# Projections by halves of TensorE's columns, steps ordered by use of the array, and turns split around the next scores

## The chip, the cores and the metric

The kernel runs on one core of one Trainium2 chip. The metric is the device time of one execution in microseconds (us); the time given for a kernel is the median of several executions. The profile is one execution recorded by the hardware profiler. A core has five engines that work at the same time and wait for each other through semaphores: PE (TensorE, matrix products; PEld is its loading of weights, that is of the operand that stands still), DVE (VectorE), ACT (ScalarE), POOL (GpSimd) and SP (which issues transfers here).

## The reference

Two blocks follow each other. The first is a linear attention with polynomial features, on 4 batches of 4 heads, 1088 tokens and 32 columns a head:

```python
def phi(x):
    a = np.einsum('rd,bhsd->bhsr', S1, x)
    b = np.einsum('rd,bhsd->bhsr', S2, x)
    return np.einsum('bhsi,bhsj->bhsij', a, b).reshape(*x.shape[:-1], r * r)
q_p, k_p = (phi(q), phi(k))
kv = np.einsum('bhsf,bhsd->bhfd', k_p, v)
z = np.sum(k_p, axis=2)
num = np.einsum('bhsf,bhfd->bhsd', q_p, kv)
den = np.einsum('bhsf,bhf->bhs', q_p, z)[..., None] + 1e-06
x = num / den
```

Its result, with the heads side by side, is the input `x` (4, 1088, 128) of the second block: four experts, each a causal softmax attention with 64 columns, of which a gate picks two for each token.

```python
logits = x @ w_gate
topk = np.argpartition(-logits, K, axis=-1)[..., :K]      # K = 2
w = softmax of the two picked logits
for e in range(E):                                        # E = 4
    q = x @ wq[e]; k = x @ wk[e]; v = x @ wv[e]
    scores = scale * (q @ k.transpose(0, 2, 1))           # causal mask, then softmax
    a = softmax(scores)
    ye = a @ v @ wo[e]
    out += ye * (w where e was picked, else 0)
```

All of it is computed in 32-bit floats.

## The kernel before

**The work of a batch.** The first block of a batch ("preparing" it) takes these steps, each a small function inside `prepare`: `begin` (DVE turns the loaded k and q), `sketch` (products with S1 and S2, then the features), `kvs` (features of k times v), `turn_features` (features of q turned on TensorE), `numer` (numerator and denominator, then the division on DVE into `xs`) and `turn_x` (that result turned into `xT`). From `xT` come the projections: `project` makes q or k of two experts for 512 tokens (tile `qk`), `project_tails` the same for the last 64 tokens (`qkt`), `project_v` the values and gate logits of 128 tokens (`vg`), and `gate` the weights of the experts.

**The units.** The second block of a batch is cut into eight units by `units`: a pair of blocks of 128 query tokens times a pair of experts. The first pair of blocks is one unit of kind Q; the second gives two units of kind P; the third and fourth give four of kind G; the last 64 tokens are one unit of kind L. The last batch takes them in another order, with Q at the end. A unit has up to two halves, x = 0 and x = 1, one for each block of queries. It goes through these stages:

- scores (`make(x)`, tiles `sc`): TensorE multiplies q and k; then DVE adds the mask and takes the maximum (`take`), and ACT takes exp and the sum (`soften`), which leaves the softmax in a tile `a`
- turns (`turns_of`, tiles `tp`): TensorE turns `a` in blocks of 128x128, two halves of rows at a time, and `evacuate` copies the result to `aT`
- values (`values`, tiles `av`): TensorE multiplies `aT` and the values
- output (`output`, tiles `po` and `acc`): the product with `wo`, and the weighting with the gate.

`evacuate` gives one copy of three to DVE and two to ACT. All results of TensorE go to one pool of eight PSUM banks.

**The order on TensorE is written out by hand.** The other engines are ordered by a planner; TensorE executes exactly in the order in which the loop at the end calls these functions. In each step of that loop, n counts the units of a batch, and the next batch is prepared in between: `ahead[n]` holds what is done for the next batch in this step, `own[n]` what is left of this batch's projections. Before the change a step is:

1. scores of both halves of the unit
2. output of the unit before the last
3. values of an earlier unit
4. `tiled`: steps of the preparation that stand on their own
5. the turns, with other steps (`own` and `between`) spread among them by `weave`, which uses a guessed time for each (the number that `piece` takes). For kinds G and L the turns of the unit itself are all done in the step; for Q and P they are done in the next step, and their values one step later still.

**How the array is used.** TensorE's array has 128 rows and 128 columns. Four uses occur here, and a profile shows them before the shape of the result: `128*128` (the whole array: `qk`, `qkt`, `vg`), `64*128` (two halves of the rows, which work on two products side by side: `sc`, `tp`, `tq`, `tx`, `po`), `128*64` (two halves of the columns: `av`, `kv`) and `64*64` (quarters: `kps`, `qps`, `num`, and the scores of kind L). Where two products go to two halves, their instructions stand one after the other and run at the same time.

Of the kernel before, what the change touches and what calls it, by code (L numbers as in the profile page):

```python
# [19 lines left out]
def kernel(  # L20
# [20 lines left out]
    nc = tc.nc  # L41
    B, H, S, D = q.shape
    R = S1.shape[0]
    DM, E = w_gate.shape
    HD = wq.shape[2]
    assert (H, D, R, E, HD, S) == (4, 32, 8, 4, 64, 1088) and H * D == DM == 128
    C = S // 32
    NJ = (S + 127) // 128
    SP = 128 * NJ
    NG = E // 2  # L50
# [36 lines left out]
    kT = const("kT", [128, SP])  # L87
    qT = const("qT", [128, SP])
# [127 lines left out]
    def prepare(b):  # L216
        first = b == 0
# [137 lines left out]
            for _ in range(n):  # L355
                nc.tensor.matmul(t, idle, idle[:, None, :].to_broadcast([128, 4, 128]), start=True, stop=True)

        def wt(a):
            return wqk[:, a // NG, 2 * (a % NG) : 2 * (a % NG) + 2, :].rearrange("p e d -> p (e d)")

        def project(a, c):
            t = bank(f"qk{b}_{a}_{c}")
            nc.tensor.matmul(t, wt(a), xT[:, 512 * c : 512 * c + 512], start=True, stop=True)  # L363
            evacuate(qk[:, a, 512 * c : 512 * c + 512], t)

        def project_tails():
            t = bank(f"qkt{b}")
            for a in range(2 * NG):
                nc.tensor.matmul(t[:, 64 * a : 64 * a + 64], wt(a), xT[:, 1024:S], start=True, stop=True)
            evacuate(qk[:, :, 1024:], t[:, 0 : 64 * 2 * NG].rearrange("p (a s) -> p a s", a=2 * NG))  # L370

        def project_v(j):
            m = size(j)
            t = bank(f"vg{b}_{j}")
            nc.tensor.matmul(t[0:m, 0 : E * HD + E], xT[:, 128 * j : 128 * j + m], wvg, start=True, stop=True)  # L375
            evacuate(vt[0:m, j], t[0:m, 0 : E * HD + E])

        def gate(j0, j1):
# [21 lines left out]
            nc.vector.tensor_tensor(out=w, in0=w, in1=tops, op=ALU.mult)  # L400


        def piece(us, f, *args):
            return us, lambda: f(*args)

        halves = ((0, 4), (4, NJ))
        sk, sq = ([piece(0.13 * (j1 - j0), sketch, nm, t, j0, j1) for j0, j1 in halves] for nm, t in (("k", kT), ("q", qT)))
        kv = [piece(2.2, lambda: (kvs(0), kvs(1)))]
        tq = [piece(0.06 * n, turn_features, y, min(y + n, 2 * NJ)) for n in ((4 if first else 8),) for y in range(0, 2 * NJ, n)]
        nu = [piece(0.25 * (x1 - x0), numer, x0, x1) for x0, x1 in (((0, 4), (4, NJ)) if first else ((0, 5), (5, NJ)))]  # L410
        cuts = ((0, 2), (2, 4), (4, 7), (7, NJ)) if first else ((0, 5), (5, NJ))
        tx = [piece(0.06 * (x1 - x0), turn_x, x0, x1) for x0, x1 in cuts]
        vg = [piece(0.43, project_v, j) for j in range(NJ)] + [piece(0.0, gate, 0, NJ)]
        pr = [[piece(0.86, project, a, c) for a in (0, 2, 1, 3)] for c in range(2)]
        pr[1].append(piece(0.8, project_tails))
        turn_in = [piece(0.0, begin), piece(0.0, begin_rest)]


        if first:

            ahead = turn_in + sk + [piece(0.0, busy, 1)] + sq[0:1] + kv + tq[0:2] + nu[0:1]
            ahead += [piece(0.0, load_next, 0)] + sq[1:] + [piece(0.0, load_next, 1)] + tx[0:2]
            ahead += pr[0][0:3] + tq[2:5] + pr[0][3:4]
            own = [nu[1:] + vg[0:4] + tx[2:] + [piece(0.0, load_next, 2)], vg[4:] + pr[1][0:1], pr[1][1:4], pr[1][4:]]
        else:
            tiled = [turn_in + sk + sq, [], kv, [], [], nu, [], []]
            if b == 1:
                tiled[0:4] = [[], [], turn_in + sk, sq + kv]
            between = [[], [], [], [], tq, [], tx + vg[0:6], vg[6:] + pr[0]]
            ahead = list(zip(tiled, between))  # L430
            own = [pr[1][0:2], pr[1][2:3], pr[1][3:4], pr[1][4:]] if b < B - 1 else [pr[1][0:2], pr[1][2:]]
        return (qk, vt, gw), ahead, own


# [97 lines left out]
        return r  # L532


    def weave(jobs, fillers):

        n, spent, total = max(len(jobs), 2), 0.0, sum(us for us, _ in fillers)
        fillers = collections.deque(fillers)
        for s in range(n):
            if s < len(jobs):  # L540
                jobs[s]()
            while fillers and (s == n - 1 or spent + fillers[0][0] / 2 <= total * (s + 1) / n):
                us, f = fillers.popleft()
                spent += us
                f()

    def units(b, qk, vt, gw):

        for p in range((NJ - 1) // 2) if b < B - 1 else (1, 3, 2, 0):
            yT = p2.tile([128, NG, 256], F32, tag="yT", name=f"yT{b}_{p}")
            z = p4.tile([128, 2, E], F32, tag="z", name=f"z{b}_{p}")
            nk = 2 * (2 * p + 2)
            four = []
            for g in range(NG):
                if p or not g:
                    aT_all = p2.tile([128, 16 * 256], F32, tag="aT", name=f"aT{b}_{p}_{g}")
                aT = aT_all[:, 0 if p else g * nk * 256 :][:, 0 : nk * 256].rearrange("p (e j s) -> p e j s", e=2, s=256)  # L560
                name = f"{b}_{p}_{g}"

                def values(p=p, g=g, aT=aT, yT=yT, z=z, name=name):
                    av = bank(f"av{name}")
                    for j in range(2 * p + 2):
                        lo = 128 * max(0, j - 2 * p)
                        for e in range(2):
                            c = HD * (2 * g + e)
                            nc.tensor.matmul(av[HD * e : HD * e + HD, lo:256], vt[:, j, c : c + HD],  # L569
                                             aT[:, e, j, lo:256], start=(j == 0), stop=(j == 2 * p + 1))  # L570

                    evacuate(yT[:, g], av[:, 0:256])
                    if g < NG - 1:
                        return []
                    share = shares(f"{b}_{p}", z, gw[:, 2 * p : 2 * p + 2])
                    return [lambda: output(b, p, yT, share)]

                def make(x, p=p, g=g, z=z):
                    return scores(b, 2 * p + x, g, qk, z[:, x, 2 * g : 2 * g + 2])

                def turns(made, x, p=p, aT=aT, name=name):
                    return turns_of(f"{name}_{x}", 2 * p + x, made[x], aT, 128 * x)

                if p == 0:
                    four.append((turns, values))
                else:
                    yield "P" if p == 1 else "G", make, turns, [values]
            if four:
                yield ("Q", lambda x, z=z: scores_first(b, qk, [z[:, :, 2 * g : 2 * g + 2] for g in range(NG)]),
                       lambda made, x: [f for g in range(NG) for i in range(2) for f in four[g][0](made[0][g], i)],  # L590
                       [values for _, values in four])
            if p == NJ // 2 - 1:
                yield last_unit(b, qk, vt, gw)
# [50 lines left out]
    with tc.manual_schedule(engines={mybir.EngineType.PE}):  # L644
# [2 lines left out]
        for _ in range(4):  # L647
            nc.tensor.matmul(warm, idle, idle[:, None, :].to_broadcast([128, 4, 128]), start=True, stop=True)
        now, ahead, own = prepare(0)
        for _, f in ahead:  # L650
            f()

        turns, turning, groups, done = [], [], [], []

        def do_values():
            nonlocal groups
            made = [f for values in groups for f in values()]
            groups = []
            return made

        for b in range(B):
            coming, ahead, later = prepare(b + 1) if b + 1 < B else (None, [], [])
            for n, (kind, make, turned, close) in enumerate(units(b, *now)):
                tiled, between = ahead[n] if n < len(ahead) else ([], [])
                made = {x: make(x) for x in ((0, 1) if kind in "PG" else (0,))}

                for f in done:
                    f()
                done = do_values()
                for _, f in tiled:  # L670
                    f()
                jobs = turns
                turns = [f for x in made for f in turned(made, x)]
                if kind in "GL":
                    jobs += turns[: len(turns) // 2]
                weave(jobs, (own[n] if n < len(own) else []) + between)
                groups += turning
                turning = []
                if kind in "GL":
                    for f in turns[len(turns) // 2 :]:  # L680
                        f()
                    turns = []
                (groups if kind in "GL" else turning).extend(close)
            now, own = coming, later
        for f in done + turns:
            f()
        groups += turning
        for f in do_values():
            f()


# [28 lines left out]
```

## Time and profile before

| what | value |
|---|---|
| time, median of 3 | 352.77 us (352.61 to 353.52) |
| span of the profiled execution | 348.0 us |
| PE busy | 324.6 us (93%), 4970 matmul instructions |
| DVE busy | 245.4 us (71%) |
| ACT busy | 236.7 us (68%) |
| POOL busy | 45.7 us (13%) |
| mean granted TensorE clock | 0.991 |

In the profile a group of instructions is named by its line, engine and operation, and by its tiles as output<-inputs. The product of two 32-bit operands is recorded as two matmul instructions, so `x8` of `qk` are four projections. The ends of matmuls are modelled and the next one begins before the end that is shown; what a matmul takes of TensorE's time is read from the distance of starts, or from the chain of waits, where a piece runs from the start of its first instruction to the start of what follows.

### The profile page before, as it was taken

The numbers are of one execution on the slowest core, as the hardware profiler recorded it, in microseconds if no ns is written. First come the engines' busy times: TensorE is split into PE (matmuls) and PEld (weight loads), VectorE is DVE, ScalarE is ACT, GpSimd is POOL, SyncE is SP. The second block draws the span as 40 slices with busy tenths as digits, with TensorE's granted clock in tenths as the row PEclk, the third lists the DMA queues.
The fourth block names the chain that finished last, engine by engine and source line by source line (L and its number), as shares of the span: only waits on it lengthen the run. The fifth ranks groups of instructions, "written<-read, shape, count | busy, mean of one in ns | idle before, by whom it ended". The sixth has DMA issues, their size and how long they took to land.

```text
span 348.0 us, 11952 instructions
## 1 busy us (share of the span) xinstructions
PE 324.6 (93%) x4970; PEld 227.0 (65%) x4970; DVE 245.4 (71%) x856; ACT 236.7 (68%) x637; POOL 45.7 (13%) x60
## 2 busy tenths in 40 slices
PE   7998999999899899999999999999989998999973
PEld 4755558777667567677665847777765655667663
DVE  6568988779457965877766756677946766767763
ACT  2447767875767576877756875986576776857782
POOL 4001047000000821000000280000000010000000
PEclk9999999999999989999999999999999999999998
DMA  7361522200000000000000000000000000000001
GB/s 206 51 179 35 180 64 83 67 4 17 16 2 3 17 6 2 18 3 18 2 17 2 11 9 6 17 2 2 18 18 3 2 15 6 3 2 17 18 7 30
DMA packets 11383, 10.22 MB, mean 29 GB/s; under 512 B 3648, under 2 KB 10304, under 8 KB 11328
## 3 DMA queue, kind: packets, MB, share of 16 engines
q1 hardware_dynamic: 11312, 9.45, 10.0%
q8 instruction: 39, 0.64, 0.8%
q14 instruction: 16, 0.13, 0.1%
q10 hardware_dynamic: 16, 0.00, 0.0%
HBM read 7.22 MB, written 2.23 MB: 27 GB/s over the span
## 4 chain that ended last, share of the span: by engine, by line
PE 54%; DVE 21%; ACT 15%; issue 9%; DMA 0%; DVEq 0%; ACTq 0%
ACT a L442 11%; PE tp L80 10%; PE sc L455 10%; PE av L569 9%; PE qk L363 8%; DVE a L437 7%; PE vg L375 4%; DVE acc L634 3%; PE po L629 2%; PE sc L496 2%; ACT acc L633 2%; PE kv L304 2%; DVE xs L338 2%; DVE aT L69 2%; PE av L609 2%
## 5 line engine op out<-in xcount | busy, mean ns | idle before, releaser
L442 ACT ACTIVATE a<-a,mx 128x256 f32<-128x256 f32 (+8 forms) x136 | 107.5, 791 | 57.5 <-DVE mx L437 57.4
L437 DVE CUSTOM_DVE_ANT_0 a<-sc,mask 128x512 f32<-128x512 f32 (+3 forms) x136 | 74.4, 592 | 13.5 <-PE sc L455 10.9
L71 ACT COPY aT<-tp 128x512 f32<-128x512 f32 (+5 forms) x146 | 61.7, 501 | 10.8 <-PE tp L80 10.1
L569 PE MATMUL av<-aT,vt 128*64 128x256 f32 (+1 forms) x640 | 67.5, 362 | 0.4 <-DVE aT L69 0.4
L80 PE MATMUL tp<-ident,a 64*128 64x64 f32 x1296 | 59.6, 229 | 8.6 <-ACT acc L633 2.6
L80 PEld LDWEIGHTS tp<-ident,a 64*128 64x128 f32 x1296 | 49.0, 138 | 26.8 <-issue 4.8
L455 PE MATMUL sc<-qkT 64*128 64x512 f32 (+3 forms) x320 | 65.3, 534 | 0.3 <-DVE acc L634 0.3
L569 PEld LDWEIGHTS av<-aT,vt 128*64 128x64 f32 x640 | 43.4, 137 | 25.9 <-DVE mx L437 3.4
L455 PEld LDWEIGHTS sc<-qkT 64*128 64x128 f32 x320 | 33.8, 191 | 20.0 <-issue 10.3
L640 POOL TENSOR_TENSOR ob<-acc 128x256 f32<-128x256 f32 (+1 forms) x19 | 12.7, 669 | 249.2 <-DVE acc L634 69.9
L69 DVE COPY aT<-tp 128x512 f32<-128x512 f32 (+6 forms) x70 | 36.4, 547 | 11.8 <-PE tp L80 11.3
L437 DVE CUSTOM_DVE_ANT_0 a<-sc,mask,mx 128x512 f32<-128x512 f32 (+3 forms) x72 | 38.2, 568 | 0.0
L634 DVE SCALAR_TENSOR_TENSOR acc<-po,r,acc 128x128 f32<-128x128 f32 (+1 forms) x72 | 20.4, 339 | 19.6 <-ACT acc L633 18.7
L363 PE MATMUL qk<-xT,wqk 128*128 128x512 f32 x64 | 32.0, 620 | 0.7 <-ACT xT L71 0.5
L442 ACT ACTIVATION_READ_ACCUMULATOR a<-a,mx 128x1 f32 x136 | 25.4, 186 | 0.0
L629 PEld LDWEIGHTS po<-wo,yT 64*128 64x128 f32 (+1 forms) x288 | 20.2, 181 | 6.1 <-issue 2.4
L375 PE MATMUL vg<-wvg,xT 128*128 128x260 f32 (+1 forms) x72 | 19.8, 403 | 2.8 <-DVE xT L69 1.8
L633 ACT ACTIVATE acc<-po,r 128x128 f32<-128x128 f32 (+1 forms) x72 | 20.6, 356 | 2.4 <-PE po L629 2.4
L629 PE MATMUL po<-wo,yT 64*128 64x128 f32 (+1 forms) x288 | 21.6, 278 | 0.4 <-ACT yT L71 0.4
L71 ACT COPY qkT<-qk 128x512 f32<-128x512 f32 x19 | 11.1, 586 | 12.9 <-PE qk L363 12.7
L529 DVE TENSOR_SCALAR r<-z 128x8 f32<-128x8 f32 x16 | 2.7, 171 | 22.0 <-ACT a L442 22.0
L437 DVE DVE_READ_ACCUMULATOR2_ANT mx<- 128x1 f32 x216 | 17.8, 83 | 0.0
(119 smaller groups left out, 329.3 us busy)
## 6 DMA issues: line engine op xcount, KB each, us to landing
kin<-in_k_dram SPq DMA_DIRECT2D x4, 544.0 KB, 3.7
qin<-in_q_dram SPq DMA_DIRECT2D x4, 544.0 KB, 4.7
vin<-in_v_dram SPq DMA_DIRECT2D x16, 128.0 KB, 4.5
out_dram<-ob SPq DMA_DIRECT2D x15, 128.0 KB, 1.8
vtl<-in_v_dram SPq DMA_DIRECT2D x8, 16.0 KB, 2.3
wqk<-in_moe_wq_dram SPq DMA_DIRECT2D x1, 128.0 KB, 4.8
wqk<-in_moe_wk_dram SPq DMA_DIRECT2D x1, 128.0 KB, 3.5
wvg<-in_moe_wv_dram SPq DMA_DIRECT2D x1, 128.0 KB, 3.4
```

Source lines behind the costliest of these rows:

```text
L69: nc.vector.tensor_copy(out_, in_)
L71: nc.scalar.copy(out_, in_)
L80: nc.tensor.transpose(ts[half][0 : in_.shape[1], 64 * x : 64 * x + 64], in_[rows], ident[rows, rows])
L363: nc.tensor.matmul(t, wt(a), xT[:, 512 * c : 512 * c + 512], start=True, stop=True)
L375: nc.tensor.matmul(t[0:m, 0 : E * HD + E], xT[:, 128 * j : 128 * j + m], wvg, start=True, stop=True)
L437: nc.vector.tensor_tensor_reduce(out=dst, in0=src, in1=msk, scale=-1.0, scalar=most, op0=ALU.add, op1=ALU.min, accum_out=mx)
L442: nc.scalar.activation(out=a, in_=a, func=ACTF.Exp, bias=mx, scale=-1.0, accum_out=z)
L455: nc.tensor.matmul(sc[e], qk[rows, g, 128 * i : 128 * i + 128], qk[rows, NG + g, keys], start=True, stop=True)
L569: nc.tensor.matmul(av[HD * e : HD * e + HD, lo:256], vt[:, j, c : c + HD], aT[:, e, j, lo:256], start=(j == 0), stop=(j == 2 * p + 1))
L629: nc.tensor.matmul(pos[e][:, x, g], yT[rows, g, 128 * x : 128 * x + nq], wo_sb[rows, g], start=True, stop=True)
L633: nc.scalar.activation(out=acc[:, x, g], in_=pos[0][:, x, g], func=ACTF.Copy, scale=s0)
L634: nc.vector.scalar_tensor_tensor(out=acc[:, x, g], in0=pos[1][:, x, g], scalar=s1, in1=acc[:, x, g], op0=ALU.mult, op1=ALU.add)
```

## The change

It has three parts.

- **Projections by halves of the columns.** `project`, `project_tails` and `project_v` made one product that used the whole array. Each is now two products that use one half of the columns each: for `qk` and `qkt` one per expert (64 columns of weights), for `vg` one per 64 tokens. They use the array as the values (`av`) do.
- **Steps ordered by use of TensorE.** The guessed times and `weave` are gone. Each step of the loop now has four lists: `tiled` (steps that use quarters), `cols` (steps that use halves of the columns; they stand just ahead of the values), `rows` (steps that use halves of the rows; ahead of the second scores) and `rows_last` (the same, after the first turns). Thus steps of one use stand together. Several steps move for this: for later batches `numer` goes from after the values to before them; `turn_x` goes ahead of the second scores, and `project_v` after them; `kvs` moves to `cols`.
- **A unit's turns split around the next scores.** The first half of a unit's turns is done at the end of its own step, the second half in the next step, between that unit's scores of x = 0 and of x = 1. This holds for all kinds of unit, and values always follow one step after the scores.

```diff
         def project(a, c):
             t = bank(f"qk{b}_{a}_{c}")
-            nc.tensor.matmul(t, wt(a), xT[:, 512 * c : 512 * c + 512], start=True, stop=True)
+            for e in range(2):
+                nc.tensor.matmul(t[64 * e : 64 * e + 64], wqk[:, a // NG, 2 * (a % NG) + e],
+                                 xT[:, 512 * c : 512 * c + 512], start=True, stop=True)
             evacuate(qk[:, a, 512 * c : 512 * c + 512], t)
...
             for a in range(2 * NG):
-                nc.tensor.matmul(t[:, 64 * a : 64 * a + 64], wt(a), xT[:, 1024:S], start=True, stop=True)
+                for e in range(2):
+                    nc.tensor.matmul(t[64 * e : 64 * e + 64, 64 * a : 64 * a + 64], wqk[:, a // NG, 2 * (a % NG) + e],
+                                     xT[:, 1024:S], start=True, stop=True)
...
             t = bank(f"vg{b}_{j}")
-            nc.tensor.matmul(t[0:m, 0 : E * HD + E], xT[:, 128 * j : 128 * j + m], wvg, start=True, stop=True)
+            for x in range(0, m, 64):
+                nc.tensor.matmul(t[x : x + 64, 0 : E * HD + E], xT[:, 128 * j + x : 128 * j + x + 64], wvg,
+                                 start=True, stop=True)
...
-            tiled = [turn_in + sk + sq, [], kv, [], [], nu, [], []]
+            ahead = {4: ([], [], [], tq), 5: (nu, [], [], []), 6: ([], vg[0:6], tx, []), 7: ([], vg[6:] + pr[0], [], [])}
             if b == 1:
-                tiled[0:4] = [[], [], turn_in + sk, sq + kv]
-            between = [[], [], [], [], tq, [], tx + vg[0:6], vg[6:] + pr[0]]
-            ahead = list(zip(tiled, between))
-            own = [pr[1][0:2], pr[1][2:3], pr[1][3:4], pr[1][4:]] if b < B - 1 else [pr[1][0:2], pr[1][2:]]
+                ahead.update({2: (turn_in + sk, [], [], []), 3: (sq, kv, [], [])})
+            else:
+                ahead.update({0: (turn_in + sk + sq, [], [], []), 2: ([], kv, [], [])})
+            own = {0: pr[1][0:2], 1: pr[1][2:3], 2: pr[1][3:4], 3: pr[1][4:]} if b < B - 1 else {0: pr[1][0:2], 1: pr[1][2:]}
+            own = {n: ([], f, [], []) for n, f in own.items()}
...
-                made = {x: make(x) for x in ((0, 1) if kind in "PG" else (0,))}
-
+                tiled, cols, rows, rows_last = (x + y for x, y in zip(own.get(n, none), ahead.get(n, none)))
+
+                made = {0: make(0)}
+                for f in turns + rows:
+                    f()
+                if kind in "PG":
+                    made[1] = make(1)
                 for f in done:
                     f()
-                done = do_values()
-                for _, f in tiled:
+
+                for f in tiled + cols:
                     f()
-                jobs = turns
+                done = [f for values in group for f in values()]
+                group = values
                 turns = [f for x in made for f in turned(made, x)]
-                if kind in "GL":
-                    jobs += turns[: len(turns) // 2]
-                weave(jobs, (own[n] if n < len(own) else []) + between)
-                groups += turning
-                turning = []
-                if kind in "GL":
-                    for f in turns[len(turns) // 2 :]:
-                        f()
-                    turns = []
-                (groups if kind in "GL" else turning).extend(close)
+                n = (len(turns) + 1) // 2
+                for f in turns[0:n] + rows_last:
+                    f()
+                turns = turns[n:]
```

More of the change, by code (lines that the diff above doesn't have):

```diff
@@ L356, in busy @@
                 nc.tensor.matmul(t, idle, idle[:, None, :].to_broadcast([128, 4, 128]), start=True, stop=True)
-        def wt(a):
-            return wqk[:, a // NG, 2 * (a % NG) : 2 * (a % NG) + 2, :].rearrange("p e d -> p (e d)")
         def project(a, c):
             t = bank(f"qk{b}_{a}_{c}")
-            nc.tensor.matmul(t, wt(a), xT[:, 512 * c : 512 * c + 512], start=True, stop=True)
+            for e in range(2):
+                nc.tensor.matmul(t[64 * e : 64 * e + 64], wqk[:, a // NG, 2 * (a % NG) + e],
+                                 xT[:, 512 * c : 512 * c + 512], start=True, stop=True)
             evacuate(qk[:, a, 512 * c : 512 * c + 512], t)
@@ L400, in gate, with piece @@
             nc.vector.tensor_tensor(out=w, in0=w, in1=tops, op=ALU.mult)
-        def piece(us, f, *args):
-            return us, lambda: f(*args)
+        def piece(f, *args):
+            return lambda: f(*args)
         halves = ((0, 4), (4, NJ))
-        sk, sq = ([piece(0.13 * (j1 - j0), sketch, nm, t, j0, j1) for j0, j1 in halves] for nm, t in (("k", kT), ("q", qT)))
-        kv = [piece(2.2, lambda: (kvs(0), kvs(1)))]
-        tq = [piece(0.06 * n, turn_features, y, min(y + n, 2 * NJ)) for n in ((4 if first else 8),) for y in range(0, 2 * NJ, n)]
@@ L410, in prepare @@
-        nu = [piece(0.25 * (x1 - x0), numer, x0, x1) for x0, x1 in (((0, 4), (4, NJ)) if first else ((0, 5), (5, NJ)))]
-        cuts = ((0, 2), (2, 4), (4, 7), (7, NJ)) if first else ((0, 5), (5, NJ))
[L412 to L415, printed above, removed]
@@ L416, in prepare @@
-        turn_in = [piece(0.0, begin), piece(0.0, begin_rest)]
+        sk, sq = ([piece(sketch, nm, t, j0, j1) for j0, j1 in halves] for nm, t in (("k", kT), ("q", qT)))
+        kv = [piece(kvs, 0), piece(kvs, 1)]
+        many = 4 if first else 8
+        tq = [piece(turn_features, y, min(y + many, 2 * NJ)) for y in range(0, 2 * NJ, many)]
+        nu = [piece(numer, x0, x1) for x0, x1 in (((0, 4), (4, NJ)) if first else ((0, 5), (5, NJ)))]
+        cuts = ((0, 2), (2, 4), (4, 7), (7, NJ)) if first else ((0, 5), (5, NJ))
@@ L419, in prepare @@
+        tx = [piece(turn_x, x0, x1) for x0, x1 in cuts]
+        vg = [piece(project_v, j) for j in range(NJ)] + [piece(gate, 0, NJ)]
+        pr = [[piece(project, a, c) for a in (0, 2, 1, 3)] for c in range(2)]
+        pr[1].append(project_tails)
+        turn_in = [begin, begin_rest]
         if first:
-            ahead = turn_in + sk + [piece(0.0, busy, 1)] + sq[0:1] + kv + tq[0:2] + nu[0:1]
-            ahead += [piece(0.0, load_next, 0)] + sq[1:] + [piece(0.0, load_next, 1)] + tx[0:2]
+            ahead = turn_in + sk + [piece(busy, 1)] + sq[0:1] + kv + tq[0:2] + nu[0:1]
+            ahead += [piece(load_next, 0)] + sq[1:] + [piece(load_next, 1)] + tx[0:2]
@@ L423, in prepare @@
             ahead += pr[0][0:3] + tq[2:5] + pr[0][3:4]
-            own = [nu[1:] + vg[0:4] + tx[2:] + [piece(0.0, load_next, 2)], vg[4:] + pr[1][0:1], pr[1][1:4], pr[1][4:]]
+            own = {0: (nu[1:], vg[0:4], [], tx[2:] + [piece(load_next, 2)]), 1: ([], vg[4:] + pr[1][0:1], [], []),
+                   2: ([], pr[1][1:4], [], []), 3: ([], pr[1][4:], [], [])}
         else:
-            tiled = [turn_in + sk + sq, [], kv, [], [], nu, [], []]
+            ahead = {4: ([], [], [], tq), 5: (nu, [], [], []), 6: ([], vg[0:6], tx, []), 7: ([], vg[6:] + pr[0], [], [])}
@@ L532, in shares @@
         return r
[L535 to L544, printed above, removed]
-                f()
     def units(b, qk, vt, gw):
@@ L649 @@
         now, ahead, own = prepare(0)
-        for _, f in ahead:
+        for f in ahead:
             f()
[L653 to L659, printed above, removed]
-        for b in range(B):
-            coming, ahead, later = prepare(b + 1) if b + 1 < B else (None, [], [])
-            for n, (kind, make, turned, close) in enumerate(units(b, *now)):
-                tiled, between = ahead[n] if n < len(ahead) else ([], [])
-                made = {x: make(x) for x in ((0, 1) if kind in "PG" else (0,))}
+        turns, group, done = [], [], []
+        none = ([], [], [], [])
+        for b in range(B):
+            coming, ahead, later = prepare(b + 1) if b + 1 < B else (None, {}, {})
+            for n, (kind, make, turned, values) in enumerate(units(b, *now)):
+                tiled, cols, rows, rows_last = (x + y for x, y in zip(own.get(n, none), ahead.get(n, none)))
[4 more added lines that the diff above has]
+                    made[1] = make(1)
                 for f in done:
                     f()
-                done = do_values()
-                for _, f in tiled:
-                    f()
-                jobs = turns
+                for f in tiled + cols:
+                    f()
+                done = [f for values in group for f in values()]
+                group = values
                 turns = [f for x in made for f in turned(made, x)]
-                if kind in "GL":
-                    jobs += turns[: len(turns) // 2]
-                weave(jobs, (own[n] if n < len(own) else []) + between)
-                groups += turning
-                turning = []
-                if kind in "GL":
-                    for f in turns[len(turns) // 2 :]:
-                        f()
-                    turns = []
-                (groups if kind in "GL" else turning).extend(close)
+                n = (len(turns) + 1) // 2
+                for f in turns[0:n] + rows_last:
+                    f()
+                turns = turns[n:]
             now, own = coming, later
@@ L686 @@
             f()
-        groups += turning
-        for f in do_values():
+        for f in [f for values in group for f in values()]:
             f()
```

## The prediction
> **What bounds the kernel now.** I read the busy shares first, then the busy times by stretch, then the chain of waits in order of time, the groups of instructions, and last what TensorE itself waited for.
>
> ```profile
> PE 324.6 (93%) x4970; PEld 227.0 (65%) x4970; DVE 245.4 (71%) x856; ACT 236.7 (68%) x637; POOL 45.7 (13%) x60
> ...
> PE 54%; DVE 21%; ACT 15%; issue 9%; DMA 0%; DVEq 0%; ACTq 0%
> ```
>
> The chain goes through PE for 54% of the span. DVE and ACT have 30% of slack each. That alone doesn't say that PE is the bound everywhere, so here are stretches of about one batch (columns: the stretch, its length, busy us of each engine with the count of instructions, the granted clock, the share of DMA, GB/s):
>
> ```profile
> 0.00:20.00 20.00, 16.38 (x460) 11.68 (x461) 13.13 (x39) 6.54 (x20) 3.63 (x23) 1.00 0.50 117
> 20.00:113.00 93.00, 89.65 (x1344) 62.11 (x1342) 70.30 (x249) 65.11 (x182) 13.31 (x11) 1.00 0.21 60
> 113.00:197.00 84.00, 80.02 (x1240) 55.66 (x1238) 60.09 (x210) 58.63 (x161) 13.15 (x11) 0.98 0.03 9
> 197.00:278.00 81.00, 78.13 (x1170) 56.00 (x1161) 55.85 (x196) 58.02 (x149) 11.83 (x9) 1.00 0.03 9
> 278.00:348.00 70.00, 60.44 (x786) 41.56 (x782) 46.02 (x166) 48.40 (x129) 3.80 (x6) 0.98 0.04 12
> ```
>
> PE lacks 3.4, 4.0 and 2.9 us in the three middle stretches, but 9.6 us in the last one, where no batch is left to be prepared and nothing fills the waits for a softmax. In all it lacks 23.4 us. So a saving on PE in the first three batches should nearly all reach the end; in the last one less. The chain of waits shows what a visit to one kind of product costs (start, length, what):
>
> ```profile
> 91.57 1.10 PE vg L375 x4
> 93.25 1.95 PE vg L375 x8
> 127.57 1.45 PE av L569 x16
> 131.61 1.05 PE qk L363 x2
> 187.52 3.63 PE qk L363 x8
> 199.98 1.91 PE qk L363 x4
> ```
>
> For `qk` the lengths 1.05, 1.91 and 3.63 us for 2, 4 and 8 instructions lie on a line: 0.43 us each and 0.19 us for the visit. For `vg`: 0.213 each and 0.25 a visit. The 0.2 us is paid whenever the use of the array changes. I also took distances of starts from the instructions in order of time: a `qk` starts 429 ns after the one before it, but the first `tp` after the last `qk` starts 523 ns after it, which is 94 ns more; the second `qk` of a visit starts 534 ns after the first, 105 ns more. The same 94 to 98 ns stand at nearly every change of use; the second extra is 104 ns for `qk`, `vg`, `sc` and `po`, about 52 ns for `tp`, `av` and `qps`, and 25 ns for `num` and `kv`. So a change costs 200, about 150 or about 120 ns by what comes first after it.
>
> ```profile
> L569 PE MATMUL av<-aT,vt 128*64 128x256 f32 x512 | 61.9, 384 | 0.4 <-DVE aT L69 0.4
> L369 PE MATMUL qkt<-xT,wqk 128*128 128x64 f32 x32 | 4.3, 278 | 0.0
> ```
>
> One `av` instruction lasts 384 ns as recorded, yet sixteen pass in 1.45 us: two halves of the columns run side by side (by the 429 ns for 512 columns, a pair over 256 takes 213 ns and one over 128 takes 107; six such pairs and two make 1.5 us). The last view is what PE waited for:
>
> ```profile
> PE tp L80 <- ACT acc L633: 2.6, 5, 0.8
> PE vg L375 <- DVE xT L69: 1.8, 2, 0.9
> PE tp L80 <- ACT yT L71: 1.6, 1, 1.6
> PE tp L80 <- DVE xs L338: 1.3, 5, 0.4
> ...
> PE vg L375 <- ACT xT L71: 1.1, 1, 1.1
> PE tp L80 <- DVE mx L437: 1.1, 2, 0.8
> ...
> PE tp L80 <- DVE den L335: 0.5, 3, 0.2
> PE tx L80 <- ACT acc L633: 0.4, 2, 0.2
> ```
>
> [...]
>
> **Part 1 and 2: halves of the columns, and fewer changes of use.** I wrote out the order of products of both kernels and counted changes among the four uses. Before: 134. Into the whole array 31 (x 200 ns = 6.2 us), into halves of the columns 30 (28 `av` x 147, 2 `kv` x 123 = 4.4), into halves of the rows 58 (48 turns x 150, 10 `sc`/`po` x 200 = 9.2), into quarters 15 (x 120 to 147 = 2.0). Sum 21.7 us. After: 93. Whole array 1 (the idle product of the start, 0.2), columns 36 (5.3), rows 41 (39 turns, 2 others: 6.3), quarters 15 (2.0). Sum 13.7 us. Saved: 8.0 us of PE time.
>
> The products themselves cost the same: two `qk` halves over 512 columns side by side take the 429 ns of one whole (taken from `av`, where a pair over 256 columns takes 213 ns). The exception is `qkt`: its 64 columns need 53 ns but follow each other by 112 ns, as each needs a load of 128 columns of weights. With 64 columns the pair can follow by 58 ns, as the `av` of the L unit do: 32 x 54 ns = 1.7 us saved. [...] I take 1.7. The number of evacuations doesn't change. Sum of PE work saved: 9.7 us.
>
> What of it reaches the end: the three middle stretches have 3 to 4 us of waits in over 80, so nearly all there; the last (70 us) and the start (20 us) have waits that swallow most. By share that is about three quarters: 7.3 us.
>
> **Part 3 and the moved steps: waits.**
> - `vg` waits for `xT`, three times, 2.9 us in all. After, the second scores (four products, 1.7 us) and often an output (1.0 us) stand between `turn_x` and `project_v`, and a copy takes 0.5 us. Gone: 2.9 us. The wait of `tx` for a bank (0.4 us) goes too.
> - `tp` behind `numer`'s DVE work (`xs`, `den`, 1.8 us): after, an `av` of 1.3 to 2.6 us stands between. I take half: 0.9 us.
> - `tp` waiting for a softmax or for banks held by outputs (`acc`, `yT`, `mx`, 5.3 us): mostly last batch, where one wait that ends at 295.3 us is 1.6 us, and others around the last Q unit are 0.8 and 0.4 us. There the turns of a half now come after the other half's scores, an output or values, so the softmax has 3 to 5 us rather than 1 to 3. Half: 2.7 us.
> - Around 116 to 127 us DVE is the bound (9.05 us busy of 11; it turns the next batch's inputs while maxima are due), PE starves and its clock falls to a mean of 0.85 there, a loss of 1.6 us. The order of DVE's work hardly changes there; I count half of the clock loss as given back, 0.8 us.
> - New waits: at a Q step `sketch` now comes ahead of the L unit's values, not after them. Its banks need ACT, which then does eight exps and four `acc` (109.5 to 114.1 us, without a gap). Up to 1 us in each of two batches, of which the values, now later, give part back. Also the copies of a second half of turns queue on DVE behind four maxima (4 x 0.6 = 2.4 us); who waits for them is the values, and the second scores and output (1.7 + 1.0 us) lie between, except in the last batch after L. I charge 1.5 us in all.
>
> Waits net: 2.9 + 0.4 + 0.9 + 2.7 + 0.8 - 1.5 = 6.2 us. Total 7.3 + 6.2 = 13.5 us, and 352.8 - 13.5 = 339.3 us.
>
> **Rivals.**
> - *Only the changes of use pay (22%).* Waits move rather than go: DVE and ACT have as much to do, in a shorter time. For it: DVE and ACT are at 70% and would rise to 73%. Against: the `xT` wait is one of order alone. Time 352.8 - 7.3 = 345.5 us.
> - *More comes back (8%).* The even spread of maxima and exps takes most of PE's 23.4 us of lack away, except for the 6 us of start: waits give 11 us, and all of the 9.7 arrives, 332 us.
> - *Slower (8%).* [...] copies of the turns behind four maxima hold banks, and the second scores wait for a bank. With 0.5 us in each of the 32 unit steps that is 16 us against 7.3 us: 361 us. Against: eight banks are four for scores and four for turns, and the scores' banks are free once the maxima are done.
> - *Halves of the columns don't overlap (2%).* 32 `qk` x 2 x 429 ns and 32 `vg` x 2 x 219 ns more, 41 us: 387 us with the savings. The `av` rows speak against it.
>
> **How the numbers follow.** The forecast has 60%, the others 22, 8, 8 and 2. The low end takes in most of the "more" case (333), the high end the first rival with a term of new waits of 3.5 us (349). Slower by over 0.3%: the last two less what ends near no change, 8%. Within 0.3%: 3%, a part of the first rival with more new waits. Faster: 89%.
>
> **What would show it.** The distance of starts of `qk` pairs should stay at 429 ns, and of `vg` pairs at 219 ns; changes of use should still cost 94 ns each; `qkt` should fall from 112 to about 58 ns a step. The waits of `vg` for `xT` should be gone, and PE should lack some 16 us rather than 23. The middle stretches should be about 3 us shorter each for work and 1 us for waits. It is wrong if PE's lack grows, with `sc` or `tp` released by DVE's copies of `aT`, or with `qps` or `qk` waiting in the Q steps.

## The result and the profile after

The changed kernel takes 370.82 us (median of 4, 366.55 to 371.35) against 352.69 us before: a ratio of 1.0508, with a 95% interval of 1.0401 to 1.0614. It is 5% slower. The prediction was 339.3 us, with a range of 333 to 349. Some executions of a kernel ran at a lower granted clock and took over 1.5% longer than its fastest (two of five of e4_explate, the profiled one among them, and two of four of e6_warm); the ratios leave these out.

The page of the changed kernel, busy times and shares of the chain by engine:

```profile
PE 333.4 (90%) x5130; PEld 231.5 (63%) x5130; DVE 247.3 (67%) x856; ACT 233.0 (63%) x637; POOL 45.8 (12%) x60
...
PE 62%; ACT 13%; DVE 12%; issue 12%; DMA 0%; POOLq 0%; DVEq 0%; ACTq 0%
```

DVE and ACT have the same work as before within 4 us. PE is busy for 8.8 us longer although its products should be cheaper, and it lacks 35.2 us of the span (368.6 less 333.4), where it lacked 23.4 before and the prediction expected 16. Busy time by stretch shows where. The stretches run from one L unit's first scores to the next, so that both kernels are cut at the same work (columns as in the prediction). First the kernel before:

```profile
0.00:96.30 96.30, 89.33 (x1600) 62.91 (x1600) 72.32 (x237) 60.49 (x170) 16.95 (x34) 1.00 0.31 81
96.30:179.70 83.40, 79.42 (x1206) 55.14 (x1204) 59.16 (x208) 58.43 (x158) 13.15 (x11) 0.98 0.03 9
179.70:261.50 81.80, 78.93 (x1212) 57.35 (x1208) 56.27 (x204) 58.64 (x157) 11.83 (x9) 1.00 0.03 9
261.50:307.30 45.80, 44.24 (x508) 27.75 (x506) 31.96 (x105) 32.21 (x75) 1.17 (x2) 1.00 0.02 5
307.30:348.00 40.70, 32.70 (x464) 23.86 (x460) 25.68 (x105) 26.95 (x81) 2.63 (x4) 0.97 0.06 16
```

Then the changed kernel:

```profile
0.00:98.80 98.80, 90.62 (x1620) 61.42 (x1620) 72.09 (x235) 58.19 (x167) 16.95 (x34) 0.98 0.30 79
98.80:185.50 86.70, 80.03 (x1250) 56.09 (x1248) 59.65 (x208) 57.61 (x158) 13.10 (x11) 0.98 0.03 9
185.50:269.40 83.90, 79.93 (x1250) 56.17 (x1248) 57.08 (x204) 56.88 (x158) 11.89 (x9) 0.98 0.03 9
269.40:316.50 47.10, 44.34 (x552) 29.35 (x550) 32.78 (x110) 32.96 (x79) 1.74 (x3) 1.00 0.02 5
316.50:368.60 52.10, 38.47 (x480) 28.52 (x476) 25.66 (x102) 27.33 (x79) 2.07 (x4) 0.89 0.04 12
```

Every stretch is longer, by 2.5, 3.3, 2.1, 1.3 and 11.4 us, which is the whole 20.6 us between the two profiled executions. More than half is in the last stretch, from the last L unit to the end, where PE is idle for 13.6 us rather than 8.0 and its clock is granted at 0.89 rather than 0.97. What PE waited for in the changed kernel (us in total, times, longest):

```profile
PE av L563 <- ACT aT L71: 11.8, 5, 3.9
PE po L623 <- ACT aT L71: 3.4, 4, 1.1
PE sc L462 <- ACT aT L71: 2.6, 3, 1.7
PE qps L272 <- ACT aT L71: 2.0, 2, 1.0
PE num L330 <- ACT aT L71: 1.4, 2, 0.7
```

All of these end with a copy of turns (`aT`) on ACT. In the same view of the kernel before, such a copy ends one wait of 0.2 us. The waits of `vg` for `xT` are gone as forecast, and so are those of `tp` for a softmax or a bank, of which half was forecast; this took their place.

The longest of these waits, instructions in order of time (start, length, engine, line, and in brackets the idle time before and what ended it):

```profile
316.53 2.06 PE L503 MATMUL sc<-qkT 64*64 64x512 f32 x24
...
317.66 0.69 DVE L444 CUSTOM_DVE_ANT_0 a<-sc,mask 128x512 f32<-128x512 f32 x1 [0.80 <-PE sc L503]
...
318.53 1.21 PE L80 MATMUL tp<-ident,a 64*128 64x64 f32 x32
...
320.45 0.28 DVE L444 CUSTOM_DVE_ANT_0 a<-sc,mask_last,mx 128x64 f32<-128x64 f32 x1
320.61 1.20 ACT L449 ACTIVATE a<-a,mx 128x1088 f32<-128x1088 f32 x1 [3.01 <-DVE mx L444]
...
320.66 1.28 DVE L69 COPY aT<-tp 128x512 f32<-128x512 f32 x2
...
321.81 1.19 ACT L449 ACTIVATE a<-a,mx 128x1088 f32<-128x1088 f32 x1
...
322.99 1.05 ACT L71 COPY aT<-tp 128x512 f32<-128x512 f32 x2
...
323.61 2.02 PE L563 MATMUL av<-aT,vt 128*64 128x256 f32 x7 [3.87 <-ACT aT L71]
```

Read it from the end. `av` waits 3.87 us for the first of two copies on ACT. The turns that they copy were done by 319.7 us. But ACT's order has the two exps of the L unit first. These need the maxima, which DVE makes from six pieces until 320.7 us. So ACT stands idle for 3.01 us with an exp at its head that cannot start, then does both exps, and only then, from 322.99 us on, the copies. The first copy starts 4.46 us after the turns do; in e4_explate below it starts 0.78 us after them. Of these 3.7 us, 1.3 go to the wait for the maxima and 2.4 to the two exps.

Just before this wait ends the granted clock falls to 0.50. Busy time and clock (the last number but two) around it, and two visits of `av` in the chain of waits, the one before the wait and the one after it:

```profile
319.00:330.00 11.00, 7.13 (x55) 4.86 (x52) 3.76 (x15) 3.43 (x6) 0.00 (x0) 0.69 0.00 0
323.00:329.00 6.00, 5.39 (x25) 3.63 (x27) 0.81 (x5) 1.04 (x3) 0.00 (x0) 0.50 0.00 0
```

```profile
312.20 3.39 PE av L563 x32
323.61 6.67 PE av L563 x31
```

A mean of 0.69 over 11 us is 6.8 us at half speed (in the trace from 322.84 to 329.66 us), and the `av` that waited takes 6.67 us where the one before it takes 3.39.

### The profile page after: what moved, and what is told of

It reads as the page before. It is cut to its first block, busy times and chain, and to the rows that moved or that the text cites. A ratio compares the mean times of both kernels' runs of the same rounds, so it can differ in the third digit from the quotient of the medians.

```text
span 368.6 us, 12267 instructions
## 1 busy us (share of the span) xinstructions
PE 333.4 (90%) x5130; PEld 231.5 (63%) x5130; DVE 247.3 (67%) x856; ACT 233.0 (63%) x637; POOL 45.8 (12%) x60
## 4 chain that ended last, share of the span: by engine, by line
PE 62%; ACT 13%; DVE 12%; issue 12%; DMA 0%; POOLq 0%; DVEq 0%; ACTq 0%
PE av L563 17%; ACT a L449 9%; PE sc L462 9%; PE qk L361 8%; PE tp L80 8%; DVE a L444 4%; PE po L623 4%; PE vg L377 3%; ACT aT L71 3%; PE num L330 2%; PE av L603 2%; PE sc L503 2%; PE kv L304 2%; PE tq L80 1%; PE kps L272 1%
## 5 line engine op out<-in xcount | busy, mean ns | idle before, releaser
L563 PE MATMUL av<-aT,vt 128*64 128x256 f32 (+1 forms) x640 | 74.5, 377 | 14.2 <-ACT aT L71 11.8
L462 PE MATMUL sc<-qkT 64*128 64x512 f32 (+3 forms) x320 | 80.3, 558 | 3.2 <-ACT aT L71 2.6
L563 PEld LDWEIGHTS av<-aT,vt 128*64 128x64 f32 x640 | 51.8, 143 | 38.0 <-ACT aT L71 15.1
L71 ACT COPY aT<-tp 128x512 f32<-128x512 f32 (+6 forms) x143 | 60.4, 478 | 16.2 <-PE tp L80 15.5
L69 DVE COPY aT<-tp 128x512 f32<-128x512 f32 (+6 forms) x73 | 39.1, 552 | 34.1 <-PE tp L80 33.9
L80 PE MATMUL tp<-ident,a 64*128 64x64 f32 x1296 | 53.9, 225 | 0.4 <-DVE aT L69 0.2
L462 PEld LDWEIGHTS sc<-qkT 64*128 64x128 f32 x320 | 35.3, 192 | 21.9 <-issue 6.9
L361 PE MATMUL qk<-xT,wqk 128*64 128x512 f32 x128 | 33.4, 623 | 0.5 <-ACT xT L71 0.5
L71 ACT COPY yT<-av 128x256 f32<-128x256 f32 (+1 forms) x25 | 9.0, 361 | 32.0 <-PE av L563 27.0
L623 PE MATMUL po<-wo,yT 64*128 64x128 f32 (+1 forms) x288 | 25.6, 284 | 3.4 <-ACT aT L71 3.4
L377 PE MATMUL vg<-wvg,xT 128*64 128x260 f32 x136 | 18.2, 391 | 0.0
```

The costliest lines, as they stand in the source:

```text
L69: nc.vector.tensor_copy(out_, in_)
L71: nc.scalar.copy(out_, in_)
L80: nc.tensor.transpose(ts[half][0 : in_.shape[1], 64 * x : 64 * x + 64], in_[rows], ident[rows, rows])
L361: nc.tensor.matmul(t[64 * e : 64 * e + 64], wqk[:, a // NG, 2 * (a % NG) + e], xT[:, 512 * c : 512 * c + 512], start=True, stop=True)
L377: nc.tensor.matmul(t[x : x + 64, 0 : E * HD + E], xT[:, 128 * j + x : 128 * j + x + 64], wvg, start=True, stop=True)
L462: nc.tensor.matmul(sc[e], qk[rows, g, 128 * i : 128 * i + 128], qk[rows, NG + g, keys], start=True, stop=True)
```

## The experiments

Each ratio is against the kernel before on the same chip.

**Halves of the columns alone (e1_halves).** The three functions of the first hunks of the diff, in the kernel before; nothing else.

> The kernel before with the projections by halves of the columns alone; order, weave and turns as before. If the halves cost what I worked out (no more time for the products, less at each change of use, qkt without its wait for weights): changes of use fall from 22.9 to 20.0 us by count, qkt gives 1.7 us, so about 348 to 350 us against 352.7. If the halves themselves are what costs time (the rival: they do not overlap fully, or twice the instructions hold PE up): above 355 us.

Measured: 345.26 us, ratio 0.9895 (0.9843 to 0.9947). The kernel before took 349.28 us on that chip, so the gain is about 3.7 us, against 4.6 us by count (22.9 - 20.0 + 1.7; the prediction had 21.7 us for the kernel before, the count made for this run 22.9). The halves are a gain, of about the size worked out; the rival, that the halves themselves cost time, does not hold.

**The whole array again, in the changed kernel (e2_whole).** The same three functions put back, in the changed kernel.

> The changed kernel with the projections put back to the whole array; order and split as changed. Theory 'split': the exps of the next unit stand ahead of the copies of the second half of turns on ACT, and values wait; the time stays with the changed kernel, plus about 5 us for the changes of use that come back (13.7 to 19.0 us by count) and 1.7 us for qkt, so 372 to 378 us. Rival 'halves': well below the changed kernel, 360 us or less.

Measured: 373.55 us, ratio 1.0666 (1.0618 to 1.0714). This is slower than the changed kernel, by about 5.5 us if both ratios are taken at 350 us, where 7 were expected. So the loss is not in the halves. The five waits of `av` for `aT` on ACT are there as well, 11.0 us in all.

**No split (e3_nosplit).** All turns of a unit in its own step; the order by use stays.

```diff
-                n = (len(turns) + 1) // 2
+                n = len(turns)
```

> The changed kernel with all turns of a unit done in its own step: no turns between the scores, everything else as changed. Theory 'split': the waits of av for ACT's aT copies (11.8 us) fall to 2 us or less, the clock stays at full speed in most places, and the time falls below that of the kernel before, to 338 to 347 us. Rival 'moved steps' (the order by use, with values, sketch and numer in new places, is what costs): it stays above 360 us.

Measured: 340.92 us, ratio 0.9759 (0.9723 to 0.9796). One line turns 5.1% slower into 2.4% faster. In its waits of PE no copy `aT` on ACT is left:

```profile
PE qps L272 <- ACT acc L627: 3.7, 2, 1.8
PE tp L80 <- ACT acc L627: 3.0, 5, 0.7
PE tp L80 <- ACT a L449: 2.3, 6, 0.6
```

The split costs 7.5% of the time before, some 26 us; the rest of the change is worth 2.4%, of which the halves alone gave 1.05% (e1_halves). Where the rest comes from, the busy times of this kernel show:

```profile
PE 316.2 (93%) x5130; PEld 220.8 (65%) x5130; DVE 246.6 (73%) x856; ACT 233.1 (69%) x637; POOL 45.8 (13%) x60
```

PE is busy for 8.4 us less than in the kernel before, and of the span of 339.0 us it lacks 22.8 us, where it lacked 23.4. So nearly all of the gain is less work on PE; other waits took the place of those that went.

**The same split, with ACT's order mended (e4_explate).** TensorE's order is that of the changed kernel. The exps of x = 0 are held back in the text until the turns are written, and queued on ACT behind the last of their copies (an order on that queue, not a wait for the copy to end).

```diff
...
-                made = {0: make(0)}
+                late[0] = []
+                made = {0: make(0)}
+                held, late[0] = late[0], None
+                on_act[0] = None
                 for f in turns + rows:
                     f()
+                with tc.issue_after(on_act[0].ins) if on_act[0] else nullcontext():
+                    for args in held:
+                        soften(*args)
```

> The changed kernel with the same order on TensorE, but on ACT the exps of x = 0 are queued behind the copies of the turns that stand between the two scores. Theory 'split by way of ACT's queue': the waits of av for ACT's copies fall from 11.8 us to under 4 us, and the time to 350 to 360 us. If the copies on DVE behind four maxima, or the later exps, matter as much: 365 us or more, with av or tp waiting for DVE or for exps instead.

Measured: 346.39 us, ratio 0.9894 (0.9846 to 0.9943); of the 352.7 us that the expectation started from this is 349 us, slightly better than expected. The waits of `av` for copies on ACT fall from 11.8 to 0.6 us. The same step as above in this kernel (the profiled execution took 351.94 us; at this step the 32 turns take 1.21 us, as they do in the changed kernel at a clock of 1.00):

```profile
307.80 1.21 PE L80 MATMUL tp<-ident,a 64*128 64x64 f32 x32
...
308.58 1.07 ACT L71 COPY aT<-tp 128x512 f32<-128x512 f32 x2 [1.70 <-PE tp L80]
...
309.88 1.20 ACT L452 ACTIVATE a<-a,mx 128x1088 f32<-128x1088 f32 x1 [0.23 <-DVE mx L444]
309.94 1.28 DVE L69 COPY aT<-tp 128x512 f32<-128x512 f32 x2
310.77 2.78 PE L568 MATMUL av<-aT,vt 128*64 128x256 f32 x12 [1.76 <-DVE aT L69]
```

ACT copies from 308.58 us on, while the maxima are still being made, and its exp starts 0.23 us after the copies end, as soon as its maximum is there. `av` still waits 1.76 us, now for a copy on DVE, which stands behind six maxima. With not one product moved on TensorE, this takes back 6.1% of the 7.5%. The 1.4% that are left, against e3_nosplit, are not explained further: a kernel whose maxima on DVE also stand behind the copies was not tried.

**Copies of the second half on DVE alone (e7_dve).** The changed kernel, with `evacuate` sending the copies of those turns to DVE only.

```diff
-        if turn[0] % 3 == 0:
+        if turn[0] % 3 == 0 or between[0]:
...
```

> The changed kernel with all copies of the second half of turns on DVE, none on ACT, so that none stands behind an exp; on DVE they still stand behind the maxima of x = 0. Theory 'ACT's queue': most of the loss goes, 348 to 356 us; what is left over against e4_explate (346.4 us) is the price of the maxima. If the loss is from any queue order, DVE's too: 362 us or more.

Measured: 358.35 us, ratio 1.0187 (1.0097 to 1.0278): between the two expectations. Of the loss 3.2% goes, and a loss of DVE's queue takes its place:

```profile
PE av L563 <- DVE aT L69: 6.6, 7, 2.1
```

So it is not exps as such. In either queue the copies stand behind work of the next unit that is not ready or is long, and the values wait: at the L unit of the last batch the turns start at 310.85 us and DVE's copies of them at 312.76, behind six maxima. This run also moves work: DVE is busy for 274.9 us rather than 247.3, so how much of what is left is the order on DVE and how much its load is not told apart. Its clock was 0.998, so what is left is not the clock.

**Idle products in the waits (e6_warm).** The changed kernel, with one or three idle products (`keep`, 128x512) ahead of the values in the five steps with the longest waits.

> The changed kernel with idle products (one, or three of 0.86 us each) just ahead of the values in the five steps where av waits longest, so that TensorE is busy in a wait that it has anyway. Theory 'waits and clock': a good part of the loss is the clock at half speed after such waits; the pieces at half speed around 323 to 330 and 354 us go, and the time falls by 3 to 6 us to 365 to 368 us. If the clock plays no part, the time stays at 371 us or rises by the products that no wait hides (up to 3 us).

Measured: ratio 1.0356 (1.0253 to 1.0460); the profiled execution has a span of 363.6 us at a clock of 0.987, where the changed kernel had 368.6 at 0.970. The gain in time is not shown: it has the direction and size of the theory, but the interval overlaps that of the changed kernel, and over all four executions the median is 367.66 us, 1.044 of the kernel before, with two (369.98 and 371.04 us) in the range of the changed kernel's own. What the profile does show is the pace after the wait, of which the idle products leave 1.07 us: the first 29 `av` take 3.52 us, where the 32 of the changed kernel take 6.67.

Executions of one and the same kernel say more. The changed kernel had spans of 364.8, 368.6 and 369.4 us at clocks of 0.979, 0.970 and 0.966; span times clock is 357.1, 357.5 and 356.8. For the kernel before the same product is 343.9 to 347.0 in 14 executions with spans of 346.8 to 352.5 us. So executions differ mainly by their clock, and by this working about 11 us of the changed kernel's profiled span are lost to the clock, against 0 to 8 us before (3 in its profile); the other 11 us or so are what remains at full clock, waits less what the first two parts save. This is an estimate from the spans and clocks, not tried apart.

**`sketch` after the turns in the Q steps (e5_sketch).** The kernel without the split still had two waits of `qps` of 1.8 us, for ACT's `acc`.

```diff
-                ahead.update({0: (turn_in + sk + sq, [], [], []), 2: ([], kv, [], [])})
+                ahead.update({0: ([], [], [], turn_in + sk + sq), 2: ([], kv, [], [])})
```

> The kernel without the split (e3_nosplit), with begin, sketch of k and sketch of q moved in the Q steps of the second and third batch from ahead of the values to after the turns. If the waits of qps for ACT (3.7 us in two waits of 1.8 us there) come from the place of sketch alone, they go, and the time falls by 2 to 4 us to 337 to 339 us. If ACT is short of time in that step wherever sketch stands, other products wait instead and the time stays within 1 us of 340.9.

Measured: 337.19 us, ratio 0.9593 (0.9516 to 0.9670), 3.7 us or, by the ratios, 1.7% less than e3_nosplit. The waits of `qps` for `acc` are gone; 1.6 us of other waits of `qps` are left. Not all of the difference is the place of `sketch`: the two kernels ran on different chips, and span times clock falls by about 2 us (336.3 to 334.5 in the profiled executions), which is what the waits lost. This is the fastest version found, 4.1% below the kernel before, with a clock of 0.997 in the profiled execution.

**The same with the split (e8_sketch).** e4_explate with `sketch` after the turns.

> The kernel with exps queued behind the copies (e4_explate), with sketch after the turns in the Q steps as in e5_sketch. If the split is worth something once ACT's queue is in order: 336 to 340 us, not slower than e5_sketch. If the split has nothing to give: slower than e5_sketch by 3 to 6 us.

Measured: 343.67 us, ratio 0.9751 (0.9678 to 0.9823), slower than e5_sketch by 1.6%, some 5.6 us (6.5 us by the medians). Even with ACT's queue in order, the split has nothing to give here, with DVE's queue as it is.

## Why the prediction was wrong

**Right: the price of a change of use, and the halves.** The chain of the changed kernel, `qk` by halves:

```profile
127.81 1.01 PE qk L361 x4
205.48 1.87 PE qk L361 x8
190.17 3.65 PE qk L361 x16
```

Twice the instructions take the time of the 2, 4 and 8 before (1.05, 1.91, 3.63 us). The two halves of a pair start 6 to 7 ns apart, and pairs of `qk` follow each other by 429 ns, those of `vg` by 219, as one whole product did before. The starts after a change of use are still 94 to 101 ns late, and the second extra of `qk` and `vg` is 51 ns in place of 104. `qkt` follows by about 58 ns a pair, as taken, where one product followed by 112 ns before; the weight load ahead of each is recorded at 138 ns for 64 columns, where it was 192 ns for 128. Counted in the traces, the use of the array changes 166 times before and 117 times after; I had 134 and 93, and the difference, 49 rather than 41, is near enough. With e1_halves (0.9895) and e3_nosplit (0.9759), the two parts pay about 8 us together, which is the 8.4 us that PE is busy for less; I had 7.3 us reaching the end, besides the waits.

**Right: which waits go.** `vg` for `xT` (2.9 us) no longer occurs. But it was not all gain: in the first batch `sc` waits 1.7 us at that place, until a copy `aT` on ACT ends.

**Wrong: "I charge 1.5 us in all" for new waits.** This is the step that failed. I saw that "the copies of a second half of turns queue on DVE behind four maxima" and priced that queue, but `evacuate` gives two of three copies to ACT, and I did not ask what stands ahead of them there. It is two exps, each behind its own maxima: in the traced case the first copy is late by 3.7 us, 1.3 of them for the maxima and 2.4 for the exps. Where an output and projections stand ahead of the values, this is partly hidden; of the 11.8 us in which `av` waits for such copies, 8.9 lie in the last batch. I had named the last batch "after L" as the exception and still charged it next to nothing. The split measured a loss of some 26 us (e3_nosplit against the changed kernel), with what it does to the clock; some 21 us of it are the order of ACT's queue (e4_explate). The queue on DVE that I did price was too cheap as well: with ACT's queue in order, 1.4% or about 5 us are left, and in the traced step `av` waits 1.76 us behind the maxima.

**Wrong: "Waits net" of 6.2 us.** Of these, 2.7 us were hoped for from the split. The rest did not come either: without the split PE lacks 22.8 us rather than 23.4, as `qps` and `tp` now wait for `acc` and for exps on ACT. Waits moved rather than went, as the first rival said at 22%.

**Wrong: the rival "Slower" had the right form and too small a chance.** It let the second scores wait for banks held by copies on DVE, 0.5 us a step, 361 us, at 8%. The waits are there (`sc`, `po`, `qps` and `num` behind `aT`, 9.4 us), but the values' waits are larger, and the copies were ACT's. The sign that I gave, that PE's lack would grow with waits for copies of `aT`, came (23.4 to 35.2 us), with ACT in the place of DVE.

**Wrong: the clock as a gain of 0.8 us.** I took one slow piece before as half given back, and did not ask what new idle time would do. There were more pieces at half speed, six of 21.9 us in all in the profile of the changed kernel against two of 5.9 us before: 11 us lost, as by the working above, rather than 3.

**Mis-sized: `sketch` ahead of the values.** I charged up to 1 us in each of two batches; in the kernel without the split it was two waits of 1.8 us, and moving it gave 1.7% by the ratios, about 2 us at equal clock (e5_sketch).

## What to carry to other kernels

Before work is put between a producer and its consumer, write out the queue of every engine on the way, not of the one that was written by hand: here copies behind the next unit's exps cost some 21 us, more than twice the 8 us that the other two parts saved. Where a planner orders the other engines, it may put an instruction first that cannot start; queueing it behind the short copies gave 6.1% without moving a product. Check first that the waits to be filled exist: without the split, PE's turns waited for an exp (`a` on ACT) for 2.3 us in all, so there was little to gain by hiding that.

## What the runs showed of the hardware that was not expected

Here the clock was a part of the bill of a wait. At the end of the wait of 3.87 us in the changed kernel TensorE's clock fell to 0.50, and it stayed there for 6.8 us, some 6 of them after the wait; with idle products in that wait (e6_warm), PE was idle for 1.07 us, and the first 29 `av` behind it took 3.52 us where 32 had taken 6.67. Over its whole profiled execution the changed kernel ran at 0.970, against 0.997 in the fastest version.

Not every drop has such a wait ahead of it. One other piece at 0.50, of 3.4 us, begins at 353.6 us, at the end of a wait of 3.38 us. But three more, of 3.4 us each, begin near 87, 118 and 258 us, and no single wait just ahead of them is longer than 1.72 us: in this trace shorter waits come before a drop, too. Nor does every drop follow a wait of this change: the kernel before has a piece of 3.4 us at 0.50 from 123.6 us, where its longest wait just ahead is 0.85 us, and the profiled execution of e4_explate, in which `av` waits for copies for 2.4 us in all, ran at 0.969, as low as the changed kernel, while three others of that kernel ran at 0.987 to 0.994. The runs do not show what decides this.
